# The opening's dummy matmuls: 54 of 108 columns in place of 48 of 121

## The chip, the core and the metric

The kernel runs on one core of a Trainium2 chip. The metric is the device time of one execution in microseconds (us); lower is better. The engines are named as the profile names them: PE (TensorE matmuls), PEld (TensorE weight loads, which overlap the matmuls), DVE (VectorE), ACT (ScalarE), POOL (GpSimd) and SP (SyncE).

## What is computed

A causal sliding-window attention (window 64) over 8 batches, 8 heads, 576 positions and head size 64 is followed by a SwiGLU feed-forward block over the 4608 tokens that come out of it.

```python
def _attn_ref(q, k, v):
    scores = scale * np.matmul(q, k.transpose(0, 1, 3, 2))
    rel = pos[:, None] - pos[None, :]
    mask = (rel >= 0) & (rel < window)          # window = 64
    scores = np.where(mask, scores, -1000000000.0)
    ...
    attn = attn / (np.sum(attn, axis=-1, keepdims=True) + 1e-09)
    return np.matmul(attn, v)

def _moe_ref(x, w_gate, w_val, w_out):          # x: 4608 x 512, d_ff = 1536
    g = x @ w_gate
    silu = g * (1.0 / (1.0 + np.exp(-g)))
    val = x @ w_val
    return (silu * val @ w_out)
```

## The kernel before, in words

The tokens are cut into 36 chunks of 128 for the attention and into 9 blocks of 512 for the feed-forward. Everything is computed in bf16 with f32 sums. A small graph class records every operation with what it reads and writes; at the end it writes out five instruction streams, one for each engine, in the order in which the operations were recorded, and puts in the semaphore waits that the data need. Nothing reorders an engine's stream: each engine does its operations in the recorded order. Later in the kernel, the order is a list written by hand (`EARLY`, `LOADS`, `SHIPS`) with a planner's times for choosing PSUM banks; the opening, in `build` (L1075), is written out operation by operation.

One recorded operation of PE is a group of matmuls. Each matmul becomes two PE instructions, a weight load and the matmul itself, and only the last matmul of a group signals a semaphore.

The opening runs in this order on PE:

- `warm` (L757) issues dummy matmuls (L765) of a zeroed tile `wz` with itself into a PSUM bank that a later operation overwrites. They wait only for the memset of `wz` on DVE. Nothing reads their result.
- `first_T` (L739) has DVE cast the first 256 rows of k (loaded by `first_loads` on SP's and ACT's queues) to bf16 (L298), then transposes them on PE (L749) and copies them to `kT` on DVE and ACT.
- `T2` (L405) transposes pairs of chunks of q or k on PE (L418) and copies them to `qT` or `kT` on ACT (L296) or DVE (L298).
- `Sa` takes two PSUM banks for the scores of a chunk, `Sbias` (L443) fills them with the mask's bias by two matmuls of 512 columns (L451), and `Sb` (L457) adds the scores by 24 small matmuls (L471 and L475) and has ACT take two exponentials (L483).
- `AVs` (L584) multiplies the exponentials of a chunk with v, by 16 matmuls of 65 columns (L595); `AVn` (L605) divides by the sums on DVE (a reciprocal, L611, and a product, L614).
- `X` (L708) transposes a finished chunk on PE (L726) and has DVE or ACT copy it to `xT`.
- `F` (L770) is the feed-forward's first half: matmuls with the gate and value weights (L790), tanh on ACT (L796), two products on DVE (L798 and L800). `O` (L807) is the second half, with matmuls at L821.

The loads of q, k, v and of the weights go out from POOL (L369, L378, L384); the later transposes of q, k and x are DMA transposes on SP's queue.

The dummies' own code is this:

```python
def warm(self, count, n=512, j=None):
    ...
        for _ in range(count):
            r = e.matmul(bank[:, 0:n], self.wz[:, 0:128], self.wz[:, 0:n], start=True, stop=True)
        return r

    self.g.op("pe", pe, reads=["wz"], writes=[bk])
```

Of the kernel before, what the change touches and what calls it, by code (L numbers as in the profile page):

```python
# [166 lines left out]
class _Kernel:  # L167
# [237 lines left out]
    def T2(self, st, x, engs):  # L405
        g = self.g
        src = (self.ks2 if x == "k" else self.qs2)[st % 2]
        dst = self.kT if x == "k" else self.qT
        z0 = (2 * st) % self.NZ
        for cc in range(2):  # L410
            bank, bk = self.bank("a")
            tb = bank[:, 0:256].bitcast(BF).rearrange("p (c j t) -> p c j t", c=2, j=2)

            def pe(e, cc=cc, tb=tb):
                for c in range(2):
                    for j in range(2):
                        for p in range(2):
                            r = e.transpose(tb[64 * p:64 * p + 64, c, j, :], src[:, 4 * cc + 2 * c + p, j, :], self.ident[:, :])  # L418
                return r

            g.op("pe", pe, reads=["ident", ("s2", x, st % 2, 0), ("s2", x, st % 2, 1)], writes=[bk])
            d = dst[:, 2 * cc:2 * cc + 2, 128 * z0:128 * z0 + 256].rearrange("p c (t j) -> p c t j", j=2)
            a = tb.rearrange("p c j t -> p c t j")
            self.copy(engs[cc], d, a, [bk], [(x + "T", z, cc) for z in (z0, z0 + 1)])
            self.drop([(bank, bk)])
# [282 lines left out]
    def X(self, n, eng="sp", kind="f", half=False):  # L708
        if n >= NCH:
            return  # L710
        g = self.g
        ix, it, u = n % 4, (n // 4) % self.NX, n % 4
        xb = self.xb[ix]
        xo = self.xT[it][:, :, 128 * u:128 * u + 128]
        xk = [("xb", ix, 0), ("xb", ix, 1)]
        if eng == "sp":
            g.op("sp", lambda e: e.dma_start_transpose(xo, xb[:, :]), reads=xk, writes=[("xT", it, u)], dma=True)
            return
        bank, bk = self.bank(kind)
        tb = bank[:, 0:256].bitcast(BF).rearrange("p (c t) -> p c t", c=4)  # L720

        def pe(e):
            for c in range(4):
                for p in range(2 if half else 1):
                    w = 64 if half else 128
                    r = e.transpose(tb[w * p:w * p + w, c, :], xb[:, 128 * c + w * p:128 * c + w * p + w], self.ident[:, :])  # L726
            return r

        g.op("pe", pe, reads=["ident"] + xk, writes=[bk])
        self.copy(eng, xo, tb, [bk], [("xT", it, u)])  # L730
        self.drop([(bank, bk)])
# [38 lines left out]
    def F(self, c, fs, lo=0, hi=512):  # L770
        g = self.g
        nf, n = len(fs), hi - lo
        w = nf * n
        xT = self.xT[c % self.NX]
        xk = [("xT", c % self.NX, u) for u in range(lo // 128, hi // 128)]
        ih = c % self.NH
        i = self.n_s % self.NS
        self.n_s += 1
        sig, uu = self.sig[i], self.uu[i]
        out = self.hT[ih][:, fs[0]:fs[0] + nf, lo:hi]  # L780
        v3 = lambda a: a[:, 0:w].rearrange("p (f t) -> p f t", f=nf)
        bs = []
        for W, wk in ((self.Wg, "Wg"), (self.Wv, "Wv")):
            bank, bk = self.bank("f")
            bs.append((bank, bk))

            def pe(e, W=W, bank=bank):
                for a, f in enumerate(fs):
                    for kk in range(NK):
                        r = e.matmul(bank[:, a * n:a * n + n], W[:, kk, f * 128:f * 128 + 128], xT[:, kk, lo:hi],  # L790
                                     start=(kk == 0), stop=(kk == NK - 1))
                return r

            g.op("pe", pe, reads=xk + [(wk, f) for f in fs], writes=[bk], cost=w * 0.0017)
            if wk == "Wg":
                g.op("act", lambda e, G=bank: e.activation(sig[:, 0:w], G[:, 0:w], ACTF.Tanh, scale=0.5), reads=[bk], writes=[("sig", i)])  # L796
        (G, gk), (V, vk) = bs
        g.op("dve", lambda e: e.scalar_tensor_tensor(uu[:, 0:w], sig[:, 0:w], 1.0, G[:, 0:w], ALU.add, ALU.mult),  # L798
             reads=[("sig", i), gk], writes=[("uu", i)])
        g.op("dve", lambda e: e.scalar_tensor_tensor(out, v3(uu), 0.5, v3(V), ALU.mult, ALU.mult),  # L800
             reads=[("uu", i), vk], writes=[("hT", ih, f) for f in fs])
        self.drop(bs)
# [272 lines left out]
    def build(self):  # L1075
        F, S, AV, X, T2, O = self.F, self.S, self.AV, self.X, self.T2, self.O
        self.loads()
        self.banks("a", [4, 5, 6, 7, 0, 1, 2, 3, 4, 5, 0, 1, 2, 3, 4, 5, 6, 7, 0, 1, 2, 3, 4, 5, 6, 7, 6, 7])
        self.warm(48, n=121)
        self.first_T(("dve", "act"))  # L1080
        s0 = self.Sa(0)
        T2(0, "q", ("act", "dve"))
        self.Sbias(s0)
        self.warm(2)
        self.Sb(s0)
        s1 = self.Sa(1, True)
        self.Sb(s1)
        T2(1, "k", ("dve", "act"))
        T2(1, "q", ("dve", "act"))
        self.start()  # L1090
        s2, s3 = self.Sa(2), self.Sa(3)
        a0, a1, a2, a3 = self.AVa(0), self.AVa(1), self.AVa(2), self.AVa(3)
        self.AVs(a0)
        self.shift(1, 0, "dve")
        self.AVn(a0)
        self.shift(2, 0, "dve")
        self.Sbias(s2)
        self.Sb(s2)
        self.AVs(a1)
        self.AVn(a1)  # L1100
        self.Sbias(s3)
        self.Sb(s3)
        X(0, "dve", "a")
        X(1, "dve", "a")
        self.warm(1, j=2)
        self.AVs(a2)
        self.AVn(a2)
        self.AVs(a3)
        self.AVn(a3)
        F(0, (0, 1), 0, 256)  # L1110
        X(2, "act", "a")
        X(3, "act", "a")
        F(0, (2, 3), 0, 256)
        F(0, (0, 1), 256, 512)
        for n in range(4):
            self.did |= {w % n for w in ("s%d", "a%d", "x%d", "Tk%d", "Tq%d")}
        self.main("F0.2-3b")
        self.free = set(range(8))
        self.g.now = dict.fromkeys(self.g.now, max(self.g.now.values()))
        for t in self.program():  # L1120
            self.pump()
            first = len(self.g.ops)
            self.main(t)
            self.at[t] = next((o for o in self.g.ops[first:] if o.eng == "pe"), None)
        self.pump()
        assert not any(self.queues)
        self.g.emit()
# [42 lines left out]
```

## Time and profile before

| what | value |
|---|---|
| median of 3 runs | 327.77 us (327.61 to 330.07) |
| the profiled execution's own time | 327.67 us |
| its span, first to last instruction | 325.9 us |
| PE busy | 320.2 us, 98% of the span |
| PEld busy | 171.0 us, 52% |
| DVE busy | 203.4 us, 62% |
| ACT busy | 135.6 us, 42% |
| POOL busy | 108.3 us, 33% |
| dummy matmuls of the opening | from 1.30 to 6.22 us |
| first feed-forward matmul (L790) | at 16.53 us |

How to read it: the span is the stretch from the first to the last instruction; the execution's own time has the start and the end around it as well. A line of the timeline gives the start, the time to the end of the last instruction of the row, the engine, the line of the kernel, the operation, the tiles that it writes and reads, and how many instructions the row stands for. In brackets stands the idle time of the engine ahead of it and what ended that; "issue" is an engine that waited for nothing that the profile shows. The chain of waits is the sequence of work that ended last, followed back from the last instruction.

### The profile page before, as it was taken

Reading aid. Unit: us, or ns where it says so; the run is one execution under the profiler, and the core shown is the slowest. Engines: PE = TensorE matmul, PEld = TensorE weight load, DVE = VectorE, ACT = ScalarE, POOL = GpSimd, SP = SyncE. Lnnn points to the kernel's source line nnn. Section 1 sums busy time; section 2 is a strip of 40 time slices with the busy share of each in tenths; the row PEclk is TensorE's granted clock in tenths of the full one; section 3 lists DMA queues with packets and bytes.
Section 4 is the critical chain, followed back from the end, with each engine's and each line's share of the span. In section 5 each row is a group of like instructions: output and inputs, shape, how many; then the busy total and the mean of one; then the engine's idle time right before and its main releaser. Section 6 shows DMA issues by size and latency. Waiting matters only on the chain.

```text
span 325.9 us, 8035 instructions
## 1 busy us (share of the span) xinstructions
PE 320.2 (98%) x3451; PEld 171.0 (52%) x3451; DVE 203.4 (62%) x351; ACT 135.6 (42%) x243; POOL 108.3 (33%) x138
## 2 busy tenths in 40 slices
PE   7999999999999999999999999999999999999996
PEld 6585578775455444544445454545454544444443
DVE  4677978745387819675757576666656566555520
ACT  2745864454454244343435252525252532322222
POOL 8999980006940501506060607060602000000000
PEclk9999999999999999999999999999999999999999
DMA  9999999999999993969999999999996211100012
GB/s 142 178 193 184 168 159 149 140 139 108 132 156 142 114 187 77 145 146 161 163 153 157 156 136 122 137 120 129 121 139 80 64 37 55 43 32 33 34 62 99
DMA packets 161571, 39.85 MB, mean 122 GB/s; under 512 B 148608, under 2 KB 157056, under 8 KB 161536
## 3 DMA queue, kind: packets, MB, share of 16 engines
q0 software_dynamic: 111056, 18.62, 80.1%
q1 hardware_dynamic: 45024, 11.22, 25.7%
q10 hardware_dynamic: 5456, 9.51, 8.3%
q8 instruction: 27, 0.44, 0.6%
q14 instruction: 8, 0.07, 0.1%
HBM read 37.75 MB, written 9.44 MB: 145 GB/s over the span
## 4 chain that ended last, share of the span: by engine, by line
PE 94%; ACT 2%; POOL 1%; DVE 1%; issue 1%; POOLq 0%
PE ps L790 57%; PE ps L821 28%; PE ps L644 3%; PE ps L471 1%; PE ps L508 1%; PE ps L726 1%; ACT pt L483 1%; PE ps L854 1%; PE ps L475 1%; PE ps L418 1%; POOL qs L378 1%; PE ps L595 1%; ACT kT L296 0%; ACT qT L296 0%; PE ps L512 0%
## 5 line engine op out<-in xcount | busy, mean ns | idle before, releaser
L798 DVE SCALAR_TENSOR_TENSOR uu<-sig,ps 128x512 bf16<-128x512 bf16 x108 | 73.9, 684 | 64.1 <-ACT sig L796 63.4
L790 PE MATMUL ps<-xT,Wg 128*128 128x512 bf16 (+1 forms) x496 | 111.3, 352 | 0.3
L790 PE MATMUL ps<-xT,Wv 128*128 128x512 bf16 (+1 forms) x496 | 111.0, 352 | 0.0
L796 ACT ACTIVATE sig<-ps 128x512 bf16<-128x512 f32 x108 | 65.0, 602 | 77.4 <-PE ps L790 77.3
L821 PE MATMUL ps<-Wo,hT 128*128 128x512 bf16 x420 | 95.4, 379 | 0.0
L800 DVE SCALAR_TENSOR_TENSOR hT<-uu,ps 128x512 bf16<-128x512 bf16 x108 | 74.2, 687 | 3.7
L790 PEld LDWEIGHTS ps<-xT,Wv 128*128 128x128 bf16 x496 | 48.5, 98 | 44.9
L369 POOL DMA_DIRECT2D kn<-in_k_dram x31 | 27.6, 896 | 127.3 <-PE ps L821 96.3
L790 PEld LDWEIGHTS ps<-xT,Wg 128*128 128x128 bf16 x496 | 46.6, 98 | 42.2 <-ACT pt L483 0.2
L821 PEld LDWEIGHTS ps<-Wo,hT 128*128 128x128 bf16 x420 | 41.0, 98 | 48.5
L828 ACT ACTIVATE ost<-ps 128x512 f32<-128x512 f32 x35 | 20.9, 597 | 90.4 <-PE ps L821 84.5
L369 POOL DMA_DIRECT2D va<-in_v_dram x40 | 35.5, 912 | 11.0 <-PE ps L821 10.9
L369 POOL DMA_DIRECT2D qn<-in_q_dram x31 | 27.9, 910 | 0.0
L671 DVE RECIPROCAL rp<-ps 128x14 f32<-128x14 f32 (+1 forms) x28 | 5.7, 203 | 31.9 <-PE ps L644 31.8
L483 ACT ACTIVATE pt<-ps 128x512 bf16<-128x512 f32 x36 | 18.9, 599 | 5.8 <-PE ps L475 5.5
L673 DVE TENSOR_TENSOR xb<-ps,rp 128x896 bf16<-128x896 f32 (+1 forms) x28 | 19.4, 692 | 1.0
L520 ACT ACTIVATE pt<-ps 128x512 bf16<-128x512 f32 x36 | 18.6, 603 | 3.2 <-PE ps L512 3.0
L644 PEld LDWEIGHTS ps<-va,pt 64*64 64x64 bf16 x888 | 10.8, 107 | 6.1 <-issue 5.5
L644 PE MATMUL ps<-va,pt 64*64 64x65 bf16 x888 | 13.4, 194 | 0.1
L529 DVE TENSOR_TENSOR pt<-pt,kmask 128x1024 bf16<-128x1024 bf16 x18 | 12.3, 684 | 0.0
L529 DVE TENSOR_TENSOR pt<-pt,mask 128x1024 bf16<-128x1024 bf16 x14 | 9.4, 685 | 0.9 <-ACT pt L483 0.9
L475 PE MATMUL ps<-qT,kT 64*64 64x64 bf16 x288 | 7.7, 194 | 0.4 <-issue 0.4
(65 smaller groups left out, 139.8 us busy)
## 6 DMA issues: line engine op xcount, KB each, us to landing
out_dram<-ost ACTq DMA_DIRECT2D x35, 256.0 KB, 2.9
va<-in_v_dram POOLq DMA_DIRECT2D x32, 128.0 KB, 6.0
kn<-in_k_dram POOLq DMA_DIRECT2D x25, 128.0 KB, 4.8
qn<-in_q_dram POOLq DMA_DIRECT2D x25, 128.0 KB, 6.0
Wg<-in_moe_w_gate_dram POOLq DMA_DIRECT2D x6, 256.0 KB, 7.3
Wv<-in_moe_w_val_dram POOLq DMA_DIRECT2D x6, 256.0 KB, 7.4
Wo<-in_moe_w_out_dram POOLq DMA_DIRECT2D x2, 768.0 KB, 19.5
qs<-in_q_dram POOLq DMA_DIRECT2D x3, 256.0 KB, 6.6
```

The costliest lines, as they stand in the source:

```text
L369: self.g.op("pool", lambda e, d=d, a=a: e.dma_start(d, a), writes=ks, dma=True, after=self.hold)
L483: g.op("act", lambda e, po=po, p=p: e.activation(po, sv[p], ACTF.Exp, scale=SCALE), reads=[bx[p][1]], writes=[pk[p]])
L520: g.op("act", lambda e, po=po, p=p: e.activation(po, sv[p], ACTF.Exp, scale=SCALE), reads=[bx[p][1]], writes=[pk[p]])
L529: self.g.op("dve", lambda e: e.tensor_tensor(pt, pt, m, ALU.mult), reads=pk + [key], writes=pk)
L644: z = e.matmul(self.psa[64 * c:64 * c + 64, o:o + 65], pt[p][rows, h, 64 * a:64 * a + 64], va[m][rows, h, 0:65], start=first, stop=phase = ...
L673: g.op("dve", lambda e, d=d, num=num, rb=rb: e.tensor_tensor(d, num, rb, ALU.mult), reads=bk + [("rp", k)], writes=xk, cost=(1.0, 0.25)[k])
L790: r = e.matmul(bank[:, a * n:a * n + n], W[:, kk, f * 128:f * 128 + 128], xT[:, kk, lo:hi], start=(kk == 0), stop=(kk == NK - 1))
L796: g.op("act", lambda e, G=bank: e.activation(sig[:, 0:w], G[:, 0:w], ACTF.Tanh, scale=0.5), reads=[bk], writes=[("sig", i)])
L798: g.op("dve", lambda e: e.scalar_tensor_tensor(uu[:, 0:w], sig[:, 0:w], 1.0, G[:, 0:w], ALU.add, ALU.mult), reads=[("sig", i), gk], writes ...
L800: g.op("dve", lambda e: e.scalar_tensor_tensor(out, v3(uu), 0.5, v3(V), ALU.mult, ALU.mult), reads=[("uu", i), vk], writes=[("hT", ih, f) ...
L821: r = e.matmul(OB[:, :], hT[:, f, 128 * u:128 * u + 128], self.Wo[:, f, :], start=(f == 0), stop=(f == NF - 1), skip_group_check=mid is no ...
L828: g.op("act", lambda e: e.activation(ost[:, :], OB[:, :], ACTF.Copy), reads=[ok], writes=[("ost", io)])
```

## The change

The first call of `warm` in `build` issues 54 dummy matmuls of 108 columns in place of 48 of 121. That is 5832 columns in place of 5808, and six matmuls (and their six weight loads) more. The order of the other instructions on every engine is the same.

```diff
         self.loads()
         self.banks("a", [4, 5, 6, 7, 0, 1, 2, 3, 4, 5, 0, 1, 2, 3, 4, 5, 6, 7, 0, 1, 2, 3, 4, 5, 6, 7, 6, 7])
-        self.warm(48, n=121)
+        self.warm(54, n=108)
         self.first_T(("dve", "act"))
         s0 = self.Sa(0)
```

## The prediction

> **What bounds the kernel now.** I read the page's busy table first, then busy time by stretch, then the chain of waits and the timeline of the first 17 us.
>
> ```profile
> PE 320.2 (98%) x3451; PEld 171.0 (52%) x3451; DVE 203.4 (62%) x351; ACT 135.6 (42%) x243; POOL 108.3 (33%) x138
> ```
>
> ```profile
> 7.00:16.50 9.50, 8.73 (x235) 5.71 (x235) 6.46 (x14) 6.30 (x12) 9.01 (x14) 1.00 1.88 178
> 16.50:325.90 309.40, 306.59 (x3174) 160.53 (x3168) 193.74 (x322) 127.80 (x229) 93.75 (x114) 1.00 1.13 120
> ```
>
> Columns of the second fence: stretch, length, then busy time of PE, PEld, DVE, ACT and POOL. From 16.5 us on PE is busy for 306.59 of 309.40 us. So whatever delays the first FFN matmul (L790, at 16.53) delays the end by the same amount, less at most the 2.8 us in which PE is idle later. The case is decided in the opening:
>
> ```profile
> 1.30 4.92 PE L765 MATMUL ps<-wz 128*128 128x121 bf16 x48 [1.30 <-DVE wz L301]
> 7.00 0.62 PE L749 MATMUL ps<-ident,ost 128*128 128x128 bf16 x8 [0.79 <-DVE ost L298]
> ...
> 13.30 0.19 PE L595 MATMUL ps<-vs,pt 128*64 128x65 bf16 x1
> 13.43 0.61 PE L451 MATMUL ps<-nmask,ident 128*128 128x512 bf16 x2
> 13.96 0.24 PE L471 MATMUL ps<-qT,kT 64*64 64x128 bf16 x2
> 13.97 0.21 PE L475 MATMUL ps<-qT,kT 64*64 64x64 bf16 x1
> 14.56 0.22 PE L475 MATMUL ps<-qT,kT 64*64 64x64 bf16 x2 [0.36 <-issue]
> ```
>
> The dummies end at 6.22 and PE then waits 0.79 us for the cast of k. That wait ends at 7.00 whatever the dummies do. The line to stare at is the last one: PE stops in the middle of the scores of chunk 3, between two matmuls of one group that waits for no semaphore. Nothing starts from 13.97 to 14.56, 0.59 us. The chain of waits goes through it:
>
> ```profile
> 14.03 0.15 PE ps L471
> 14.18 0.38 issue
> 14.56 0.22 PE ps L475 x2
> ...
> 14.97 0.55 PE ps L726 x8
> 15.53 0.22 PE ps L765
> 15.74 0.37 PE ps L595 x15
> 16.11 0.04 issue
> 16.15 0.44 PE ps L595 x16
> 16.59 1.85 PE ps L790 x16
> ```
>
> and the DMA view names a likely cause, the queue that brings instructions:
>
> ```profile
> q8 instruction: 27, 0.44, 0.6%
> ```
>
> ```profile
> q0 software_dynamic: 571, 0.20, 157.0%
> q8 instruction: 1, 0.02, 5.4%
> ```
>
> The first of the two is the whole run, the second the stretch 12.2 to 13.3 us. 0.44 MB over PE's 3451 + 3451 instructions is 64 bytes each, and 0.44 MB in 27 packets is 16 KB each: PE's program comes in blocks of 256 instructions. One such packet moves in 12.2 to 13.3 (none in 0 to 12.2), between 571 packets of the loads. I take the stall at 13.97 as PE running off the end of a block while the next one is still on its way.
>
> **The change part by part.**
>
> *Columns and end of the dummies.* 48 x 121 = 5808 columns become 54 x 108 = 5832. The pitch now is (4.92 - 0.22) / 47 = 0.100 us. For 108 columns the row bounds it at 0.100 x 108/121 = 0.089 (if columns set it) and 0.100 (if each instruction costs the same). I take 0.089: the later rows follow columns, with (0.62 - 0.22) / 7 = 0.057 us for 128 columns and 0.22 us between the starts of the two 512-column matmuls of L451. The dummies then end at 1.30 + 53 x 0.089 + 0.22 = 6.24, at worst 6.82, against 6.22 now. Both are before 7.00. The cover is the wait for DVE's cast (6.27 + 0.69 = 6.96); if that were gone, each 0.1 us would cost 0.1 us. Cost: 0. The six extra weight loads lie beside the matmuls (PEld is busy 4.75 us inside PE's 4.92). No other engine's order changes, no wait or DMA is added, and only the first dummy waits.
>
> *The clock.* Early dummies run at half rate: 0.100 us for 121 columns, against 0.057 for 128 at 7.00. Their records take 308 ns until 5.5 us and 217 ns at 6.0, so the rate doubles at about 5.9 us, 4.6 us after the first. The stretch of dense work is the same 4.9 us. Cost: 0 taken; from 0 to 2.4 us if the release slips (rival D).
>
> *Twelve instructions more.* Six matmuls and their six weight loads come ahead of everything else in PE's stream, so every block boundary falls 12 instructions earlier in the program. Counted back from the stall: 7 instructions of the scores of chunk 3 were issued (L471 twice, L475 once, then one weight load, by the timeline), ahead of them 4 of the bias matmuls L451, ahead of these the 32 of AVs(a1), L595. 7 + 4 + 1 = 12: the boundary will fall just ahead of the very last matmul of AVs(a1), the one that signals DVE. Now that matmul starts at 13.30.
>
> When does the next block arrive? Counted 256 back from the stall, the boundary before it lies in the scores of chunk 0: 7 + 4 + 32 + 48 + 4 + 32 + 32 + 32 + 48 = 239, four separate waits, and the rest from the end of that group. Its 48 instructions start at 9.09 to 9.35, released by DVE's copy of qT. Twelve earlier is still in that group, so if the fetch starts when a boundary is crossed, it starts at most 0.06 us earlier, and the block is there at about 14.5 as now.
>
> So PE stops at 13.30 instead of 13.97 and goes on at 14.5 to 14.56. Behind the stall then lie, in place of the rest of the scores, first the last L595, the two L451 matmuls and the first part of the scores. Now these take from 13.30 to 13.97, 0.67 us. That is the delay, less the 0.06: 0.6 us. Bounds: +0.67 if the block lands when it does now; 0 if the stall keeps its length of 0.59 and simply lies earlier (PE would be at the same point at the same time).
>
> Who waits behind it: the scores feed ACT's two exponentials (15.01, 1.09 us), these AVs(a3) at 16.15, and that the first L790 at 16.53. Each starts within 0.1 us of its releaser, so nothing swallows the 0.6. On DVE, the reciprocal of a1 moves from 14.00 to about 14.8 and its product (0.69 us) ends at about 15.7 instead of 14.92. X(1)'s transposes, now at about 15.1 and then at 15.7 to 15.8, move by the same amount. No second delay adds up. Weight loads keep their times and get 0.6 us more slack. Later boundaries move by 12 too; from 16.5 us on the view of PE's waits lists none at all, so I take 0.1 either way.
>
> *Sum.* 0 + 0 + 0.6 on the profiled execution's own 327.67 us (span 325.9 and 1.8 around it) is 328.3. The median of the three runs is 0.10 above that execution, so 328.4.
>
> [...]
>
> **The rivals.**
>
> *B. Nothing moves* (327.8 us). Either the stop is a fixed price of crossing, 0.59 us wherever it falls, or blocks come in time and the stop has another cause that stays at L475. For: only one stop without a releaser is that long in the whole run, so its nature rests on one case. Against: later boundaries fall among equally short matmuls (L644) and PE shows no such stop there, which a fixed price would give.
>
> *C. Faster* (327.2 to 327.4 us). If the request for the block now stands behind a wait (that for ks, whose transposes start at 10.38, or that for ACT's qT, 0.37 us of idle PE before 12.68), 12 instructions earlier would put it ahead of that wait. The block then lands up to 0.9 us sooner. It decides from 0.6 us sooner on, where PE gains more than the 12 instructions' 0.67 us lose. The gain ends at the 0.38 us of the chain or the 0.59 of the stop. Against: the count puts the boundary well inside the scores of chunk 0.
>
> *D. The clock is released later* (330.1 us). On the chain, PE's pieces from 7.00 to 9.55 add up to 0.62 + 0.57 + 0.54 + 0.43 + 0.41 = 2.57 us; at half rate they would add up to about 2.4. For: one of the three runs took 330.07, 2.3 us over the median, which fits but has no trace. Against: dense time and columns are the same within 0.4%, so the change itself gives no reason.
>
> [...]
>
> **How the numbers follow.** Forecast (boundary moves, block lands as now): 0.5, 328.1 to 328.8 by itself. B 0.25, C 0.09, D 0.16. The time is the forecast's, 328.4. The range takes in C at the bottom and D's 330.1 at the top, since D's 0.16 with the tails of the others is more than 2 in 10: 327.2 to 330.1. About 1% (3.3 us) is what a measurement of this kernel can tell from no change; only a D in which the clock stays low past 9.6 us goes over it, 0.03, and nothing I can find gives 3.3 us back, 0.01. Within 1%: 0.96.
>
> **What would show it.** L765 x54 ending at 6.2 to 6.3 and L749 at 7.00: the dummies cost nothing. A stop "issue" ahead of L595 or L451 from 13.3 to about 14.5, none in L475, and the first L790 at 17.1: the forecast. A stop still inside L475 or one that ends at 13.9, and L790 at 16.5: B. No stop, and L790 at 16.1: C. L749 rows of 0.9 us or more: D. It would be wrong in its core if the stop does not move by 12 instructions.

## The result, and the profile after

The changed kernel took 328.92 us (median of 22 runs, 327.82 to 330.60) against 327.70 us before (22 runs, 327.06 to 330.07). The ratio is 1.0043, 95% interval 1.003 to 1.0055: 0.3 to 0.55% slower, within the 1% to which the prediction gave 0.96. Two more measurements of the same pair of kernels gave 1.0011 (0.9991 to 1.003) and 1.0028 (1.0009 to 1.0046). The lowest times of the three sets lie 0.6 to 0.8 us above those of before (327.82, 327.83 and 327.73 against 327.06, 327.22 and 327.05), the medians 0.77 to 1.22 us. The ratios, and the medians here and in the table, leave out executions that were disturbed (up to 1169 us); a ratio is not the quotient of two medians, and the two differ by up to 0.2%.

The profiled execution after is one of the longest, 330.60 us with a span of 328.9. Its opening on PE, from the timeline:

```profile
1.30 5.04 PE L765 MATMUL ps<-wz 128*128 128x108 bf16 x54 [1.30 <-DVE wz L301]
7.00 0.75 PE L749 MATMUL ps<-ident,ost 128*128 128x128 bf16 x8 [0.66 <-DVE ost L298]
...
11.75 0.64 PE L418 MATMUL ps<-ident,qs 128*64 128x128 bf16 x16 [0.61 <-DMA qs<-in_q_dram]
12.71 0.44 PE L595 MATMUL ps<-va,pt 128*64 128x65 bf16 x16 [0.32 <-DMA va<-in_v_dram]
...
14.24 0.20 PE L595 MATMUL ps<-vs,pt 128*64 128x65 bf16 x1
15.57 0.19 PE L595 MATMUL ps<-va,pt 128*64 128x65 bf16 x1 [1.13 <-issue]
15.69 0.61 PE L451 MATMUL ps<-nmask,ident 128*128 128x512 bf16 x2
```

Three things are to be seen. The dummies end at 6.34 and the transposes of k start at 7.00 as before, so the dummies themselves cost nothing. The stop without a releaser stands ahead of exactly one L595, the last of its group, where it stood inside L475 before: 12 instructions earlier in the program. And this execution had late loads: qs and va kept PE waiting for 0.61 and 0.32 us, which they did not before. The first L790 starts at 18.22 in place of 16.53.

A second stop of the same kind appears later, one that the profile of before does not have:

```profile
49.62 0.60 PE L790 MATMUL ps<-xT,Wv 128*128 128x256 bf16 x4
50.84 0.61 PE L790 MATMUL ps<-xT,Wv 128*128 128x256 bf16 x4 [0.61 <-issue]
```

Within a group of eight matmuls, PE stops after four, and what follows waits for no semaphore. The pause between starts is about 0.9 us where 0.11 is normal. Some matmul records are missing from this trace (3421 of 3457), so short pauses among L790 and L821 are not read; this one also shows on DVE: an L798 starts at 50.72 in place of 49.03, the next L798 at 52.99 in place of 50.51, 0.8 us later still than the opening had made it.

### The profile page after: what moved, and what is told of

The parts are those of the page before. It is cut to its first block, busy times and chain, and to the rows that moved or that the text cites. A ratio compares the mean times of both kernels' runs of the same rounds, so it can differ in the third digit from the quotient of the medians.

```text
span 328.9 us, 8011 instructions
## 1 busy us (share of the span) xinstructions
PE 317.4 (97%) x3421; PEld 171.3 (52%) x3457; DVE 203.4 (62%) x351; ACT 135.7 (41%) x243; POOL 108.6 (33%) x138
## 4 chain that ended last, share of the span: by engine, by line
PE 92%; DMA 2%; issue 2%; ACT 2%; POOL 1%; DVE 1%; POOLq 0%
PE ps L790 56%; PE ps L821 27%; PE ps L644 3%; DMA va<-in_v_dram 2%; PE ps L471 1%; PE ps L726 1%; PE ps L854 1%; PE ps L508 1%; PE ps L595 1%; ACT pt L520 1%; POOL qs L378 1%; PE ps L475 0%; PE ps L418 0%; PE ps L512 0%; ACT kT L296 0%
## 5 line engine op out<-in xcount | busy, mean ns | idle before, releaser
L798 DVE SCALAR_TENSOR_TENSOR uu<-sig,ps 128x512 bf16<-128x512 bf16 x108 | 73.9, 684 | 64.9 <-ACT sig L796 64.2
L790 PE MATMUL ps<-xT,Wv 128*128 128x512 bf16 (+1 forms) x486 | 110.7, 351 | 1.1 <-issue 0.6
L790 PE MATMUL ps<-xT,Wg 128*128 128x512 bf16 (+1 forms) x479 | 107.8, 351 | 2.7 <-issue 1.4
L821 PE MATMUL ps<-Wo,hT 128*128 128x512 bf16 x413 | 94.5, 379 | 0.5 <-ACT pt L483 0.2
L790 PEld LDWEIGHTS ps<-xT,Wv 128*128 128x128 bf16 x496 | 48.5, 98 | 45.7 <-issue 0.9
L790 PEld LDWEIGHTS ps<-xT,Wg 128*128 128x128 bf16 x496 | 46.6, 98 | 42.1 <-ACT pt L520 0.2
L821 PEld LDWEIGHTS ps<-Wo,hT 128*128 128x128 bf16 x420 | 41.0, 98 | 48.5
```

Source lines behind the costliest of these rows:

```text
L821: r = e.matmul(OB[:, :], hT[:, f, 128 * u:128 * u + 128], self.Wo[:, f, :], start=(f == 0), stop=(f == NF - 1), skip_group_check=mid is no ...
```

## The experiments

All comparisons are with the kernel before on the same chip. The first L790 and the stops are read from one profiled execution of each; the ratios come from many runs. Two theories stood against each other. By the *block theory* only the number of PE instructions ahead of a place counts: PE's program would come in blocks of 256 (the author's estimate from the page of before, 0.44 MB in 27 packets of the instruction queue over 6902 PE instructions), and PE would stop where a block ends and the next has not landed. By the *columns theory* it is 108 columns in place of 121, or the clock, that costs.

| kernel | PE instructions added | first L790, us | ratio (95%) | median, us | before beside it, us |
|---|---|---|---|---|---|
| after | 12 | 18.22 | 1.0043 (1.003 to 1.0055) | 328.92 | 327.70 |
| 48 of 108 | 0 | 16.53 | 1.0015 (0.9993 to 1.0038) | 328.42 | 327.80 |
| 54 of 121 | 12 | 16.91 | 1.002 (1.0002 to 1.0037) | 328.27 | 327.80 |
| 96 of 61 | 96 | 15.96 | 1.0031 (1.0002 to 1.0059) | 328.11 | 327.80 |
| after, again | 12 | 17.04 | 1.0011 (0.9991 to 1.003) | 328.57 | 327.80 |
| 12 added behind the stop | 12, later | (disturbed) | 1.0032 (1.0006 to 1.0058) | 328.54 | 327.46 |
| after, 12 taken out behind the stop | 12, then 0 | 16.99 | 1.0031 (1.0016 to 1.0046) | 328.12 | 327.46 |
| 51 of 114 | 6 | 16.24 | 1.0024 (1.0009 to 1.0038) | 327.90 | 327.46 |
| 17 of 342 | -62 | 16.52 | 1.0019 (1.0011 to 1.0028) | 328.13 | 327.46 |
| 12 added behind the stop, again | 12, later | 16.64 | 1.0022 (1.0009 to 1.0036) | 327.86 | 327.39 |
| 88 of 66 | 80 | 16.18 | 1.0029 (1.0008 to 1.005) | 327.96 | 327.39 |
| before, against itself | 0 | 16.20 | 1.0008 (0.9993 to 1.0022) | 327.45 | 327.39 |
| after, third time | 12 | 16.93 | 1.0028 (1.0009 to 1.0046) | 328.19 | 327.39 |

**Columns and count apart.** Two kernels change one of the two numbers each.

```diff
-        self.warm(48, n=121)
+        self.warm(48, n=108)
```

> Count theory (what matters is how many PE instructions stand ahead of the scores of chunk 3, since that sets where a 256-instruction block of PE's program ends): 48 dummies as before, so the stop without a releaser stands in the second L475 of the scores of chunk 3 as before, and the time is that of before, ratio 0.999 to 1.001 (327.7 us). Columns theory (what matters is 108 columns in place of 121, or the clock): the dense work ends at 1.30 + 47 x 0.091 + 0.2 = 5.8 us, ahead of the 5.9 us at which the rate doubled; the time is that of the changed kernel or worse, 328.9 us to 331, and the L749 rows last longer than the 0.62 us of before.

```diff
-        self.warm(48, n=121)
+        self.warm(54, n=121)
```

> Count theory: 54 dummies, so the boundary stands ahead of the last L595 of AVs(a1) as in the changed kernel, whatever their columns. Dummies end at about 6.6 us, still ahead of 7.00. Ratio 1.003 to 1.0055 as for the changed kernel (328.7 to 329.5 us). Columns theory: with 121 columns the time is that of before, ratio 0.999 to 1.001.

With 54 of 121 the stop is where the changed kernel has it, and the late stop is there too:

```profile
13.29 0.20 PE L595 MATMUL ps<-vs,pt 128*64 128x65 bf16 x1
14.26 0.19 PE L595 MATMUL ps<-va,pt 128*64 128x65 bf16 x1 [0.77 <-issue]
...
48.32 0.60 PE L790 MATMUL ps<-xT,Wv 128*128 128x256 bf16 x4
49.13 0.61 PE L790 MATMUL ps<-xT,Wv 128*128 128x256 bf16 x4 [0.21 <-issue]
```

With 48 of 108 there is neither; the first L790 starts at 16.53. The expected stop in L475 was missed as well: a wait for va had made PE 0.35 us late (L451 at 13.78 in place of 13.43), and its scores of chunk 3 then run from 14.32 without a pause, in the block theory because the block was there. The L749 rows took 0.62 us as before, so the matmuls ran at their later rate by 7.00 here too, although the dummies ended at 5.34 in place of 6.22. The columns theory falls by the places of the stops. The times say less: 1.0015 and 1.002 can't be told apart, the first lies a little above the 0.999 to 1.001 expected and the second below the 1.003 to 1.0055.

**The same kernel again.** The late loads of the first profile had to be told from the change.

> The changed kernel once more, for a second profile. If the loads of the first profiled execution were late by chance (its time of 330.6 was the longest of 22), the stop ahead of the last L595 ends at 14.5 to 15.0, no wait for qs or va stands ahead of it, and the first L790 starts at 17.1 to 17.6. If late loads belong to the change, the stop ends at 15.5 again and L790 starts at 18.2. Time 328.9 us either way, ratio 1.003 to 1.0055.

> The changed kernel on the same chip as the three others, since its first two measurements gave 1.0043 and 1.0011. Two stops of 0.4 to 0.6 and 0.4 to 0.8 us over before give 0.8 to 1.4 us, ratio 1.0025 to 1.0043; a single stop would give 0.5 us, ratio 1.0015.

From the timelines, the second profile of the changed kernel (four lines) and its third (two lines):

```profile
13.29 0.20 PE L595 MATMUL ps<-vs,pt 128*64 128x65 bf16 x1
14.38 0.19 PE L595 MATMUL ps<-va,pt 128*64 128x65 bf16 x1 [0.90 <-issue]
...
48.44 0.60 PE L790 MATMUL ps<-xT,Wv 128*128 128x256 bf16 x4
49.66 0.61 PE L790 MATMUL ps<-xT,Wv 128*128 128x256 bf16 x4 [0.62 <-issue]
```

```profile
13.38 0.20 PE L595 MATMUL ps<-vs,pt 128*64 128x65 bf16 x1
14.27 0.19 PE L595 MATMUL ps<-va,pt 128*64 128x65 bf16 x1 [0.69 <-issue]
```

The stop stands ahead of the same matmul each time and ends at 14.38 and 14.27, a little ahead of the 14.5 to 15.0 expected, with no wait for qs or va ahead of it. So the late loads belonged to that one execution, and the packet of instructions came about a microsecond late together with them. The ratio of the second measurement, 1.0011, lies below the 1.003 to 1.0055 expected. The DMA view of the first profile has the packet of instructions after 13.2, as against 12.2 to 13.3 before:

```profile
q0 software_dynamic: 592, 0.22, 153.9%
q8 instruction: 1, 0.02, 4.9%
```

(stretch 13.2 to 14.4; none in 12 to 13.2). The late stop is there in the second profile, 0.62 us, and not in the third, although the third ratio, 1.0028, is what two stops were expected to give; that profile is one of the faster executions (327.93 us, median 328.19).

**Is the late stop a thing of its own?** One kernel takes the 12 instructions out again behind the first stop, another puts 12 in there only.

```diff
-        V F0.4 F0.5 F0.6 k2t q2t F0.7 S4 F0.8 H4.1.1/act H5.0.1/act B4 F0.9 X4/act+ k3t A5 N5 F0.10 X5/act+ q3t F0.11 S6
+        V F0.4 F0.5 F0.6 k2t q2t F0.7 S4 F0.8 H4.1.1/act H5.0.1/act B4 F0.9 X4/act k3t A5 N5 F0.10 X5/act q3t F0.11 S6
...
-        self.warm(48, n=121)
+        self.warm(54, n=108)
...
-        self.warm(1, j=2)
+        self.warm(3, n=171, j=2)
```

> The changed kernel's dummies (54 of 108), and 12 PE instructions taken out again behind the first stop: the transposes of chunks 4 and 5 in 4 whole matmuls in place of 8 half ones, and the later dummy of 512 columns as 3 of 171. Block theory: the stop ahead of the last L595 stays (first L790 0.4 to 0.6 us later than before where the loads come in time), the one near 50 us goes; 0.5 us more than before, ratio 1.001 to 1.002. Rival (the second stop follows from the later opening): it stays, and the time is the changed kernel's, ratio 1.003 to 1.0055.

```profile
13.30 0.19 PE L595 MATMUL ps<-vs,pt 128*64 128x65 bf16 x1
14.33 0.19 PE L595 MATMUL ps<-va,pt 128*64 128x65 bf16 x1 [0.83 <-issue]
```

The first stop is as in the changed kernel, the first L790 at 16.99, and this profile's view of PE's waits lists no other "issue" than these 0.8 us. From the first L790 to the end of the span it takes 326.4 - 16.99 = 309.4 us, as before (325.9 - 16.53 = 309.4). The opening alone is shown here: 0.46 us later than the profile of before, and the whole span 0.5 us longer. That taking the 12 out removes the late stop is not shown by this one profile, since the changed kernel's third has none either. The ratio, 1.0031, is above the 1.001 to 1.002 expected and no smaller than the changed kernel's second and third.

```diff
-        self.warm(1, j=2)
+        self.warm(7, n=73, j=2)
```

> The dummies of the start as before (48 of 121); the later dummy of 512 columns ahead of AVs(a2) becomes 7 of 73, so 12 PE instructions are added behind the first stop and ahead of the second place (the gate or value matmuls L790 at about 49 us, where the profiles with 54 dummies have a stop of 0.5 to 0.9 us between starts and those with 48 have none). Block theory: the opening as before (first L790 at 16.5, the stop in L475), and a stop among the L790 near 49 us in this profile as in the changed kernel's, exactly at the instruction 1473; 0.4 to 0.8 us more than before, ratio 1.001 to 1.0025. Rival (the second stop is an echo of the later opening, or the columns' doing): none there, ratio 0.999 to 1.001.

The profile of this kernel is that of the execution of 1169 us, so only its other times are read. A second set of runs of it:

> The kernel of f1 once more (48 dummies of 121; the later dummy as 7 of 73, so 12 PE instructions added behind the first stop), because the profile of f1 showed a disturbed execution of 1169 us. Block theory: opening as before (first L790 at 16.4 to 16.6), and a stop of 0.4 to 0.9 us between two L790 near 49 us, at PE's instruction 1473. Rival: no stop there, the second one follows from the later opening. Ratio 1.001 to 1.004 against 0.999 to 1.001.

```profile
13.96 0.21 PE L475 MATMUL ps<-qT,kT 64*64 64x64 bf16 x1
14.67 0.22 PE L475 MATMUL ps<-qT,kT 64*64 64x64 bf16 x2 [0.47 <-issue]
```

The first stop is back in L475, as expected. The late one is not there: that expectation was missed in this profile. Its times are above before all the same (1.0022 and 1.0032, intervals above 1), so some executions of it lose time that the profiled one does not. Adding 12 there is not shown to make the late stop; with 12 added ahead it appeared in three profiles of four.

**Other places for the boundary.** If the block theory holds, the boundary can be put where it hurts less.

```diff
-        self.warm(48, n=121)
+        self.warm(51, n=114)
```

> 5814 columns in 51 dummies: 6 PE instructions more than before, half the change's. Block theory: the boundary stands one instruction inside the scores of chunk 3, behind the two bias matmuls L451, so the stop ends at 14.5 as before with only 6 short instructions more behind it: first L790 within 0.1 us of before. A theory in which the loss grows evenly with the count gives 0.25 us there. The second place lies 6 instructions earlier than before: between 0 and 0.8 us there. Ratio 0.999 to 1.003.

```profile
13.43 0.61 PE L451 MATMUL ps<-nmask,ident 128*128 128x512 bf16 x2
14.24 0.24 PE L471 MATMUL ps<-qT,kT 64*64 64x128 bf16 x2 [0.21 <-issue]
```

Half of the change's instructions put the stop behind the two L451 and cost nothing in the opening: the first L790 starts at 16.24, 2.00 us behind the end of the stop, against 1.97 in the profile of before. A loss that grows evenly with the count would have given 0.25 us. It is a step, and the step lies between 6 and 12 instructions, where the bias matmuls and the last L595 get behind the boundary.

```diff
-        self.warm(48, n=121)
+        self.warm(96, n=61)
```

> 5856 columns in 96 dummies: 96 PE instructions more than before. Count theory: the boundary 256 ahead now lies among the dummies themselves, ahead of the wait for k at 7.00, so the next block is asked for before 6.3 us and lands about 5.3 us later, at 11.6, while it is needed in the scores of chunk 2 at 12.7. No stop without a releaser from 12.6 to 16 us, first L790 about 0.4 to 0.6 us earlier than before, 327.1 to 327.3 us, ratio 0.998 to 0.999. Columns theory with the same total of columns: as before. If each dummy has a floor of 0.1 us whatever its columns, they end at 10.9 us and the time is about 4 us more.

```profile
15.96 1.05 PE L790 MATMUL ps<-xT,Wg 128*128 128x256 bf16 x8
16.84 1.04 PE L790 MATMUL ps<-xT,Wv 128*128 128x256 bf16 x8
17.71 0.22 PE L726 MATMUL ps<-ident,xb 128*128 128x128 bf16 x1
18.25 0.56 PE L726 MATMUL ps<-ident,xb 128*128 128x128 bf16 x7 [0.32 <-issue]
```

The stop at 13.97 is gone and the first L790 is 0.57 us earlier than in the profile of before, as expected. Then most of it is given back at the next boundary: one transpose of L726 goes through, seven wait. By counting, the 256 instructions ahead of this stop went from 12.0 to 17.7 us, and PE goes on at 18.25. The expected gain in time was missed (1.0031).

```diff
-        self.warm(48, n=121)
+        self.warm(88, n=66)
```

> 5808 columns in 88 dummies: 80 PE instructions more than before, 16 fewer than with 96 of 61. Block theory: the boundary lies in the scores of chunk 2; the one 256 ahead lies in the transposes L418 of q at 7.6, so the block lands at about 12.9, 0.2 us after the scores of chunk 2 can start; no stop in the scores of chunk 3; the boundary after it falls into the first L790 behind the transposes of chunks 2 and 3, where PE has matmuls of 0.1 us each queued. First L790 0.3 to 0.5 us earlier than before and no stop of 0.3 us at the transposes of chunk 2 as 96 of 61 showed. Time 0.3 to 0.5 us less than before in the profile, ratio 0.998 to 1.001 with later boundaries open. Rival (more dummies cost by their count): slower than the changed kernel.

The first L790 starts at 16.18, 0.35 us earlier, but the first row of L790 behind the transposes takes 1.30 us in place of 1.04: by counting, the boundary falls behind its first matmul, as expected. The next row of L790 starts at 19.53 in place of 19.60, so 0.07 us of the gain are left by then. The time did not get better (1.0029).

```diff
-        self.warm(48, n=121)
+        self.warm(17, n=342)
```

> 5814 columns in 17 dummies: 62 PE instructions fewer than before. Block theory: the boundary comes 62 later, at the later dummy ahead of AVs(a2), so all the scores of chunk 3 and the transposes of chunks 0 and 1 go ahead of it; the boundary 256 ahead falls at the end of the scores of chunk 1 (10.2 us), so the block lands at about 15.5, when AVs(a2) starts anyway. First L790 at 16.0 to 16.2 in place of 16.5, and the next block (asked for at 15.5, there at 21) is not needed before 25. Time 0.3 to 0.5 us less than before, ratio 0.9985 to 0.999, unless a later boundary falls badly (0.4 to 0.8 us). Columns theory: as before.

```profile
15.53 0.22 PE L595 MATMUL ps<-vs,pt 128*64 128x65 bf16 x1
15.89 0.22 PE L595 MATMUL ps<-va,pt 128*64 128x65 bf16 x1
```

The scores of chunk 3 now run through, and the boundary stands behind the first matmul of AVs(a2): 0.36 us between two starts that are at most 0.05 apart elsewhere in the group. The expected gain was missed, first L790 at 16.52. The boundary ahead lies 62 instructions later in the program too, and PE goes on at 15.89 in place of 14.56.

**How far two measurements of one program lie apart.**

> The kernel before against itself, to see how far two measurements of one program lie apart: ratio 0.999 to 1.001. The block theory says its profile shows the stop in L475 at instruction 450 and none among the L790 near 49 us.

The ratio of before against itself is 1.0008. Its second profile has the first L790 at 16.20, without a listed stop in L475: the next score matmuls start at 14.25, 0.28 us behind the last one at the same place, so PE went on 0.3 us earlier than in the first profile. That is the spread of one kernel's opening.

No version was found that beats the kernel before.

## Why the prediction was right, and where a size was off

The range, 327.2 to 330.1 us, holds the time before as well, so that 328.92 lies in it says little. What carries the prediction is where the stop went and what it cost.

*Columns and end of the dummies: right.* In the first profile they end at 6.34 (predicted 6.24), ahead of 7.00. The last matmul's record is still a slow one of 0.30 us there, so the pitch was (5.04 - 0.30) / 53 = 0.089 us, the lower bound.

*Twelve instructions: right, and the core of it.* The boundary fell ahead of the very last L595 of AVs(a1) in all three profiles of the changed kernel, and in the two others with 54 dummies. Four further places, 6, 62, 80 and 96 instructions away, fell where the count puts them. The count to the boundary ahead was off without harm: it left out the two L451 of chunk 1 at 9.47 (4 instructions) and took four separate waits where the trace has three, so that boundary lies 10 instructions ahead of the end of the scores of chunk 0 in place of 13, and 12 earlier is still inside them. Rival B's fixed price is refuted: PE's idle time at the stops of the opening goes from 0.21 to 1.13 us, and where the loads were in time and the stop is listed behind instruction 449, it goes from 0.21 to 0.90 us while the stop ends at 14.24 to 14.67. Rival C's case did not occur at 12 instructions.

*0.6 us in the opening: right.* The four profiles with 54 dummies and loads in time have the first L790 at 17.04, 16.93, 16.91 and 16.99, mean 16.97. Before has 16.53 and 16.20, mean 16.37. The difference is 0.60 us, but two profiles of one kernel that lie 0.33 us apart don't fix it to better than some 0.2 us. The work behind the stop is steadier. From the end of the stop to the first L790 it takes 2.65 to 2.66 us in all five profiles with 54 dummies (14.38 to 17.04 in the second one of the changed kernel), and 1.95 to 1.97 us in the three with the stop in L475 (14.56 to 16.53 in the first one of before):

```profile
16.53 1.05 PE L790 MATMUL ps<-xT,Wg 128*128 128x256 bf16 x8
17.04 1.05 PE L790 MATMUL ps<-xT,Wg 128*128 128x256 bf16 x8
```

That is 0.69 us more, where the prediction had 0.67. DVE follows as worked out: its reciprocal of a1 moved from 14.00 to 14.61 in the second profile (14.8 was predicted), after 0.55 us of idle that ends on L595:

```profile
14.61 0.21 DVE L611 RECIPROCAL rc<-ps 128x8 f32<-128x8 f32 x1 [0.55 <-PE ps L595]
```

*"The block is there at about 14.5 as now": too narrow.* Over the profiles with 54 dummies the stop ended at 14.26 to 15.57, over those with the stop in L475 at 14.25 to 14.67. The 15.57 came with late loads; what makes the rest of the spread is not shown.

*"I take 0.1 either way" for the later boundaries: the term that was too small.* From the first L790 to the end of the span, the profile of before takes 309.4 us. The changed kernel takes 310.7, 310.1 and 309.3, the one with 54 of 121 takes 310.2. So later places cost 1.3, 0.7, -0.1 and 0.8 us, about 0.7 in the mean, with the stop among the L790 near 49 us as the piece that the traces name. The view of before's waits listed no such place, and that was taken for a price; this place, which PE passes there 3.0 us behind the packet's end (below), does not show in it. Opening and later part together are 0.6 + 0.7 = 1.3 us, against 0.8 to 1.2 by the medians and 0.4 to 1.4 by the ratios of the three measurements.

The same kernel loses nothing there in some executions, and the packet for that block differs between them. It took 1.9 us in the first profile of the changed kernel and 1.85 us in the second, which have the late stop, and 1.06 us in its third, which has none:

```profile
q8 instruction: 1, 0.02, 5.7%
q8 instruction: 1, 0.02, 5.1%
```

The first line is the first profile from 47.3 to 49.4 us (5.7% of 16 engines over 2.1 us is 1.9 us), the second the third profile from 45.2 to 46.5. In the first profile of before the packet took 1.06 us too, and by counting PE passed that boundary 3.0 us behind the packet's end. With 12 instructions more ahead and a packet of 1.06 us, in the changed kernel's third, it passed about 2.3 us behind. At the stops PE goes on 1.3 to 1.6 us behind a packet's end, so by this estimate the twelve instructions took about 0.7 us of a slack of some 1.5. In the first and the second profile, with the stop, the packet lasts 0.8 to 0.9 us longer than in the third and also starts 0.8 to 1.0 us later as measured against PE's first L566 row there, together more than the 0.8 us left of it. Why it lasts longer in some executions stays open. DMA transposes and loads moved beside it with and without a late stop (queue q1 moved 230 and 245 packets a us with it, 225 and 229 without), so they alone don't tell; taking them away was not tried.

*Rival D* struck in small: the moment at which the matmuls get faster varies. In the profile of before it lies at about 5.9 us, among the dummies. In the first profile after, the first L749 matmuls still ran slow (0.75 us for the row in place of 0.62, the longest record 314 ns in place of 229; 0.71 us and 294 ns in the third), and in the second the dummies took 4.36 us in place of 5.04, so there it came earlier, by 5.65. One kernel has both, and what sets the moment is not shown. The granted clock in the views is 1.00 ahead of it and behind it (1.3 to 5.9, 5.9 to 7 and 7 to 16.5 us in the profile of before), so that it is a clock that is released was the author's reading. The cost seen was 0.13 us, far from 2.4.

*Most boundaries cost nothing that the profile lists.* In the profile of before PE passes 26 of the 27 that can be counted without a listed stop. The exceptions are one boundary in the opening, with 0.2 to 1.1 us of idle PE in the profiles that list it, and the late place in three profiles, with 0.2 to 0.6 us.

What stays open: the kernels with 51 of 114, 17 of 342 and 12 added later have profiles as good as before, but their medians are 0.4 to 1.1 us above it. One profiled execution does not show where the others lose that.

## What to carry to other kernels

Filler instructions are not free because the engine is idle there: here six more dummies, over at 6.34 us where PE's next work came at 7.00, moved a stop by their 12 instructions, and the opening took 0.6 us longer. A pause with no releaser in the middle of a group that waits for nothing is worth counting back from, here in blocks of 256, above all where many short matmuls follow each other (256 instructions went in 4.7 us in this opening). When such a kernel changes by a few instructions, look at every boundary that has little slack, and take several profiles before reading half a microsecond.

## What the runs showed that was not expected

The stops can be numbered. Counted in PE's stream with its separate semaphore instructions, the fifteen stops of these profiles, in the opening and at the late place, stand behind instruction 449, 705 or 1473, which are 256 and three times 256 apart. PE goes on 1.3 to 1.6 us after the end of a packet of the instruction queue at the stops where that end was read: at 14.56 behind 13.2 in the profile of before, at 15.57 behind 14.24 and at 50.84 behind 49.29 in the first one after, at 14.38 behind 13.0 and at 49.66 behind 48.2 in the second. At none of the boundaries counted in the profiles of before and the first after does it pass sooner than 1.3 us behind the packet. The end of the stop also moves with the crossing of the boundary before: with 96 dummies (crossing at 7.0) PE passes the next boundary at 12.0 without a stop, in the profile of before (9.25) it goes on at 14.56 and with 17 dummies (10.4) at 15.89.

In the opening it takes 5.3 to 6.3 us from the crossing of the boundary before to the restart of PE: 9.25 to 14.56 in the profile of before, 10.4 to 15.89 with 17 dummies, 9.31 to 15.57 in the first one after. Ahead of the late stop of the first one after it took 7.9 (42.94 to 50.84). The opening uses a block up in about the same time (9.25 to 13.97 in the profile of before), so moving a boundary mostly moves the stop to the next one, as 96 of 61 showed. The crossing times are by counting, since the profile marks no boundary; 7.0 and 10.4 are the times of those places in the profile of before.

The tuned kernel sits at a good place: of eight other arrangements that were run besides the change none was faster, and those with an interval above 1 lie 0.2 to 0.3% higher.
